# Single gate, weight and output steps on the other engine, GpSimd memsets between the attention's two output stages, and a new fixed order

## The chip, the core and the metric

The kernel runs on one core of one Trainium2 chip. The engines that matter are TensorE (PE, matmuls; PEld is its weight load), VectorE (DVE), ScalarE (ACT), GpSimd (POOL) and SyncE (SP, which issues the DMAs here). The metric is device time in microseconds (us), the median of several runs. Between the runs of the kernel before the spread is 519.86 to 521.3 us.

## The reference

Two parts follow each other. The first is a gated linear attention over 768 tokens for 4 batches and 8 heads of width 48:

```python
for t in range(S):
    state = alpha[:, :, t, :, None] * state + np.einsum('bhd,bhe->bhde', k[:, :, t], v[:, :, t])
    y[:, :, t] = np.einsum('bhd,bhde->bhe', q[:, :, t], state)
```

Its output, laid out as 3072 tokens of 384, is the input `x` of a two-layer network:

```python
h = x @ w_in                                            # 384 x 2048
sp = np.maximum(h, 0.0) + np.log1p(np.exp(-np.abs(h)))
g = h * erf(sp)
return (g @ w_out).astype(np.float32)                   # 2048 x 384
```

q, k, v and alpha come as float32. The two weights come with 8 bytes a number and are turned into float32 parts on the chip.

## The kernel before

**Tiling.** The attention is cut into 24 chunks of 64 positions (two alternating sets, `M`, of 12). Two chunks make one block of 256 tokens for the network, so there are 12 blocks. A block has 4 groups of 512 hidden units, and each group is handled in two halves: a half of `h` is 128x512, a group is 128x1024. Every factor of a matmul is split into a high and a low part (`x_hi`, `x_lo`, `wi_hi`, `wi_lo`, `gh`, `gl`, `wo_hi`, `wo_lo`), and three products are added: hi by hi, the weight's low part by hi, and the weight's high part by lo.

**Steps.** All work is written as small steps with a name and indices. For a chunk: `la lk lq lv` load, `sb` and `sa` are scans over the decays, `rc` and `ic` a reciprocal and its copy, `kk qq td ta` products, `pn` transposes k on PE and `kn` copies the result to SBUF (ACT), `ps` makes the scores, `mk` masks them into `sT` (DVE), `pu` makes the state's update, `qt` and `sv` add the state's part and the scores' part of the output into the PSUM tile `py`, and `xh`, `xl` split `py` into `x_hi` (ACT) and `x_lo` (DVE). For a block: `hm_b_g_half` is the first matmul (18 instructions), `he` copies its PSUM half to `hs` (ACT), `u n1 n2 n3` and `g` are activations on 128x1024 (ACT), `ma mb z1 z2` arithmetic on 128x1024 (DVE), `ga` casts half of `hs` to `gh` (ACT), `gl` makes the rest `hs - gh` (DVE), `om` is the second matmul (12 instructions), `oe` scales and copies the sum in PSUM to `o` (ACT), `od` stores it. For a piece of the weights: `wl` loads, `wc wy wv wa wb` unpack, `wh` takes the high part (ACT), and `wq`, or `wp` on PE with `we` on ACT, the low part; the pieces' low-part steps end in `i` for `w_in` and `o` for `w_out`. `dw` issues matmuls whose result is not used. `f1`, `f2`, `f3` gather a test of the attention's numbers at the very end: on its result the program branches to a slow exact path, which is not taken with these inputs.

**What sets the order.** The text `ORDER` lists all steps once; the program issues them in that order. `Queue` (line 202) ties each instruction of PE, DVE, ACT and SP to the one before it on the same engine, so each of these engines runs exactly in the list's order, and an engine waits when its next instruction's input is not there. GpSimd is not in it. The buffers are rings: 2 of `gh`, 2 of `gl`, 7 of `hs`, 5 of `s`, 4 of `w`, 2 PSUM tiles `h`, one `py`, one `both`, one `kn`, one `sT`. In the profile nearly every instruction has line 210, the call in `Queue`, so groups are told apart by their tiles; names such as `h__111` and `h__112` are the two buffers of one ring. `need` inserts an `ACT_TABLE_LOAD` whenever ACT's next function (`n1 n2 n3` against `u` and `g`) belongs to the other of two table sets.

**Places that the change touches.** `outputs` with `qt` and `sv` (lines 354 to 407): `qt` always opens `py` (`start`), `sv` always closes it (`stop`), except in the first chunk of each set, which has `sv` alone. `kn`, `he`, `oe`, `wy`, `wh`, `we` hold one ACT instruction each. `ga` and `gd` do the same cast on ACT and on DVE; the old list names only `ga`.

Of the kernel before, what the change touches and what calls it, by code (L numbers as in the profile page):

```python
# [20 lines left out]
PSUM = bass.MemoryType.PSUM  # L21
NOSYNC = mybir.DependencyInfo(mybir.DependencyClass.NoSync, mybir.DependencyReason.DATA)
# [3 lines left out]
RT2 = 2.0**0.5  # L26
# [4 lines left out]
la_0 sb_0 wli_1 wci_1 rc_0 wyi_1 ic_0 sa_0 wli_3 wyi_3 wai_1 wbi_1 wci_3 wlo_2 wco_2 wyo_2 whi_1 dw_13 wpi_1  # L31
wai_3 wbi_3 wlo_0 wco_0 wyo_0 whi_3 wpi_3 wao_2 wbo_2 who_2 wao_0 wli_4 wci_4 wyi_4 lk_0 kk_0 wei_3 wbo_0 who_0
pn_0 kn_0 wei_1 la_1 sb_1 wai_4 lq_0 qq_0 wbi_4 wli_2 wyi_2 wci_2 wli_7 whi_4 wqo_2 wci_7 wli_8 wyi_7 wqo_0
wci_8 dw_8 ps_0 wyi_8 wai_2 wbi_2 whi_2 mk_0 dw_1 wpi_4 wei_4 lv_0 dw_2 pu_0 wli_6 wyi_6 wci_6 wai_7 lk_1 wai_8
wpi_2 wei_2 wli_0 wbi_7 whi_7 rc_1 lq_1 wbi_8 whi_8 wai_6 wyi_0 sa_1 sv_0 xh_0 dw_1 wpi_7 wei_7 lk_2 kk_1 wci_0
wbi_6 whi_6 qq_1 wai_0 wli_5 wyi_5 ic_1 wlo_9 wci_5 xl_0 wpi_8 wbi_0 wei_8 whi_0 ps_1 mk_1 wai_5 wpi_6 wei_6
lv_1 sv_1 la_2 ta_0 wlo_12 wli_11 wvo_9 wvo_12 wyo_9 wbi_5 wao_9 wyo_12 wao_12 wpi_0 wli_10 pn_1 wbo_9 whi_5
xh_1 xl_1 sb_2 wbo_12 wei_0 wli_9 wpi_5 rc_2 td_2 wci_11 who_9 wqo_9 wyi_11 sa_2 wai_11 wei_5 wlo_1 who_12
wqo_12 wlo_11 kn_1 lk_3 hm_0_0_0 hm_0_0_1 kk_2 lq_2 wbi_11 he_0_0_0 wyi_10 lv_2 qq_2 wlo_8 wci_10 wai_10
hm_0_2_0 wco_1 pu_1 la_3 sb_3 he_0_0_1 wyi_9 wlo_3 lq_3 wbi_10 qt_2 ps_2 mk_2 u_0_0 ic_2 rc_3 whi_11 wqi_11  # L40
he_0_2_0 whi_10 wqi_10 wyo_1 wao_1 wci_9 sa_3 ta_1 wvo_8 wai_9 n1_0_0 hm_0_1_0 he_0_1_0 wbo_1 td_3 wbi_9 qq_3
sv_2 xh_2 xl_2 hm_0_2_1 he_0_2_1 who_1 wqo_1 pn_2 wyo_8 wao_8 kk_3 hm_0_1_1 wlo_6 kn_2 wbo_8 n2_0_0 wvo_11 whi_9
he_0_1_1 qt_3 pu_2 wqi_9 ps_3 mk_3 ta_2 hm_0_3_0 n3_0_0 ma_0_0 wyo_6 wyo_11 wao_11 g_0_0 ic_3 lq_4 mb_0_0
he_0_3_0 la_4 sb_4 lv_3 sv_3 xh_3 xl_3 rc_4 wco_6 who_8 wqo_8 wao_6 sa_4 wbo_11 hm_0_3_1 he_0_3_1 qq_4 lv_4
z1_0_0 u_0_2 wco_3 lk_4 kk_4 hm_1_0_0 wyo_3 pn_3 kn_3 he_1_0_0 td_4 wbo_6 la_5 wao_3 u_0_1 n1_0_1 hm_1_0_1
z2_0_0 hm_1_1_0 qt_4 he_1_1_0 he_1_0_1 sb_5 pu_3 ps_4 mk_4 ta_3 n2_0_1 who_11 wqo_11 who_6 n3_0_1 ga_0_0_0
n1_0_2 ic_4 lv_5 wbo_3 lk_5 ma_0_1 gl_0_0_0 td_5 rc_5 mb_0_1 wqo_6 n2_0_2 sa_5 ga_0_0_1 gl_0_0_1 n3_0_2 ma_0_2
wlo_10 wvo_10 who_3 wqo_3 mb_0_2 wyo_10 hm_1_2_0 he_1_2_0 hm_1_1_1 he_1_1_1 sv_4 xh_4 xl_4 pn_4 lq_5 qq_5 wlo_7
g_0_1 z1_0_1 wlo_4 ic_5 om_0_0_0 g_0_2 hm_1_2_1 wao_10 z1_0_2 kk_5 z2_0_2 z2_0_1 wlo_15 he_1_2_1 wlo_5 kn_4
wyo_7 wco_7 u_0_3 lq_7 n1_0_3 hm_1_3_0 he_1_3_0 om_0_0_1 ga_0_2_0 gl_0_2_0 hm_1_3_1 ga_0_2_1 wco_4 qt_5 wbo_10  # L50
wlo_13 pu_4 la_6 wao_7 n2_0_3 who_10 ps_5 mk_5 ta_4 om_0_2_0 gl_0_2_1 sv_5 he_1_3_1 wqo_10 wbo_7 n3_0_3 ma_0_3
wyo_4 xh_5 xl_5 wyo_5 wco_5 g_0_3 wao_5 wbo_5 om_0_2_1 who_5 wao_4 mb_0_3 wbo_4 ga_0_1_1 wqo_5 who_7 who_4 wqo_7
gl_0_1_1 wvo_15 ga_0_1_0 wyo_15 hm_2_0_0 he_2_0_0 wqo_4 sb_6 u_1_0 n1_1_0 hm_2_0_1 he_2_0_1 wyo_13 om_0_1_1
gl_0_1_0 om_0_1_0 z1_0_3 hm_2_2_0 wlo_14 wao_15 z2_0_3 wbo_15 wvo_14 n2_1_0 rc_6 wvo_13 ga_0_3_0 gl_0_3_0 wao_13
# [88 lines left out]
def gla_moe(ctx: ExitStack, tc: tile.TileContext, q, k, v, alpha, w_in, w_out, out):  # L143
# [119 lines left out]
    for t in Ts[0] + Ts[1]:  # L263
# [645 lines left out]
```

## Time and profile before

| | |
|---|---|
| median of 3 runs | 519.88 us (519.86 to 521.3) |
| the profiled execution | 519.62 us, of which the span is 517.9 us |
| granted TensorE clock | 1.0 (2.4 GHz) in every stretch |
| busy: PE, PEld, DVE, ACT, POOL | 506.5, 482.4, 463.0, 487.8, 4.4 us |
| the chain that ended last | PE 78%, DVE 11%, ACT 7%, issue 2%, DMA 2%, POOL 1% |
| table loads on ACT | 58 of 1283 ns |

The rows come from one execution of 519.62 us. Matmuls overlap in the profile: a row's duration is longer than the distance from its start to the next one's start, and for what PE costs the distance is the thing to read. On DVE and ACT too, an instruction whose input does not come from the one just before it starts a little before that one ends. Idle time in front of an instruction stands in brackets behind its row, with what ended it.

### The profile page before, as it was taken

Reading aid. Unit: us, or ns where it says so; the run is one execution under the profiler, and the core shown is the slowest. Engines: PE = TensorE matmul, PEld = TensorE weight load, DVE = VectorE, ACT = ScalarE, POOL = GpSimd, SP = SyncE. Lnnn points to the kernel's source line nnn. Section 1 sums busy time; section 2 is a strip of 40 time slices with the busy share of each in tenths; the row PEclk is TensorE's granted clock in tenths of the full one; section 3 lists DMA queues with packets and bytes.
Section 4 is the critical chain, followed back from the end, with each engine's and each line's share of the span. In section 5 each row is a group of like instructions: output and inputs, shape, how many; then the busy total and the mean of one; then the engine's idle time right before and its main releaser. Section 6 shows DMA issues by size and latency. Waiting matters only on the chain.

```text
span 517.9 us, 16807 instructions
## 1 busy us (share of the span) xinstructions
PE 506.5 (98%) x7465; PEld 482.4 (93%) x7465; DVE 463.0 (89%) x590; ACT 487.8 (94%) x696; POOL 4.4 (1%) x19
## 2 busy tenths in 40 slices
PE   6899999999999999999999999999999999999996
PEld 6589999999999999999999999999999999999995
DVE  6999999999999999986899998798887988869784
ACT  7999999999998999899996999999999999999992
POOL 3000000000000000000000000000000000000000
PEclk9999999999999999999999999999999999999999
DMA  8994134412130133111113041023103012000000
GB/s 326 380 334 135 54 122 135 123 50 84 59 117 24 57 100 79 60 45 37 57 58 97 5 152 45 23 84 93 44 1 119 23 59 71 23 34 1 0 32 34
DMA packets 21389, 43.70 MB, mean 84 GB/s; under 512 B 2368, under 2 KB 5440, under 8 KB 21312
## 3 DMA queue, kind: packets, MB, share of 16 engines
q1 hardware_dynamic: 21312, 42.59, 25.1%
q8 instruction: 59, 0.97, 0.8%
q14 instruction: 18, 0.15, 0.1%
HBM read 37.86 MB, written 4.72 MB: 82 GB/s over the span
## 4 chain that ended last, share of the span: by engine, by line
PE 78%; DVE 11%; ACT 7%; issue 2%; DMA 2%; POOL 1%; DVEq 0%; POOLq 0%; ACTq 0%
PE acc L210 34%; PE h__112 L210 16%; PE h__111 L210 16%; PE py L210 5%; PE both L210 5%; PE warm L210 1%; DMA s__86<-in_moe_w_out_dram 1%; DVE t L210 1%; ACT w__97 L210 1%; DVE B L210 1%; DVE w__97 L210 1%; ACT w__100 L210 1%; DVE w__100 L210 1%; ACT wi_lo L210 1%; DVE A L210 1%
## 5 line engine op out<-in xcount | busy, mean ns | idle before, releaser
L210 ACT ACT_TABLE_LOAD x58 | 74.4, 1283 | 1.9 <-PEq L863 0.9
L210 PE MATMUL acc<-wo_hi,gh__102 128*128 128x384 f32 x192 | 44.3, 344 | 0.0
L210 PE MATMUL acc<-wo_hi,gh__101 128*128 128x384 f32 x192 | 43.2, 345 | 0.8 <-ACT gh__101 L210 0.8
L210 PE MATMUL acc<-wo_hi,gl__104 128*128 128x384 f32 x192 | 43.6, 339 | 0.1
L210 PE MATMUL acc<-wo_lo,gh__102 128*128 128x384 f32 x192 | 43.1, 337 | 0.0
L210 PE MATMUL acc<-wo_lo,gh__101 128*128 128x384 f32 x192 | 41.8, 337 | 0.0
L210 PE MATMUL acc<-wo_hi,gl__103 128*128 128x384 f32 x192 | 41.6, 337 | 0.0
L210 PEld LDWEIGHTS acc<-wo_hi,gl__104 128*128 128x128 f32 x192 | 34.1, 188 | 0.9 <-DVE gl__104 L210 0.7
L210 DVE TENSOR_TENSOR_SCAN B<-raw_a,back 128x520 f32<-128x520 f32 x24 | 29.7, 1236 | 5.5 <-POOL T L264 3.9
L210 PEld LDWEIGHTS acc<-wo_lo,gh__102 128*128 128x128 f32 x192 | 34.4, 188 | 0.0
L210 PEld LDWEIGHTS acc<-wo_lo,gh__101 128*128 128x128 f32 x192 | 34.3, 188 | 0.0
L210 PEld LDWEIGHTS acc<-wo_hi,gh__101 128*128 128x128 f32 x192 | 32.1, 188 | 2.4 <-ACT gh__101 L210 1.7
L210 PEld LDWEIGHTS acc<-wo_hi,gl__103 128*128 128x128 f32 x192 | 34.2, 188 | 0.1
L210 PEld LDWEIGHTS acc<-wo_hi,gh__102 128*128 128x128 f32 x192 | 32.7, 188 | 0.7
L210 DVE TENSOR_TENSOR_SCAN A<-raw_a,start 128x520 f32<-128x520 f32 x24 | 29.7, 1236 | 0.1
L210 PE MATMUL h__111<-x_hi__108,wi_hi 128*128 128x256 f32 x144 | 22.1, 289 | 0.0
L210 PE MATMUL h__111<-x_hi__107,wi_hi 128*128 128x256 f32 x144 | 22.0, 288 | 0.0
L210 PE MATMUL h__112<-x_hi__107,wi_hi 128*128 128x256 f32 x144 | 21.8, 287 | 0.1
L210 PE MATMUL h__112<-x_hi__108,wi_hi 128*128 128x256 f32 x144 | 21.7, 286 | 0.0
L210 PE MATMUL h__112<-x_lo__109,wi_hi 128*128 128x256 f32 x144 | 21.2, 282 | 0.2 <-issue 0.2
L210 ACT ACTIVATE s__88<-s__88 128x1024 f32<-128x1024 f32 x20 | 21.2, 1060 | 0.1
L210 DVE TENSOR_TENSOR sT<-both,mask 128x512 f32<-128x512 f32 x24 | 16.3, 681 | 5.6 <-PE both L210 5.6
(301 smaller groups left out, 1432.1 us busy)
## 6 DMA issues: line engine op xcount, KB each, us to landing
raw_a<-in_alpha_dram SPq DMA_DIRECT2D x24, 260.5 KB, 3.1
raw_k<-in_k_dram SPq DMA_DIRECT2D x24, 256.0 KB, 3.2
raw_q<-in_q_dram SPq DMA_DIRECT2D x24, 256.0 KB, 3.6
raw_v__113<-in_v_dram SPq DMA_DIRECT2D x12, 256.0 KB, 3.3
raw_v__114<-in_v_dram SPq DMA_DIRECT2D x12, 256.0 KB, 4.0
out_dram<-o__105 SPq DMA_DIRECT2D x12, 192.0 KB, 2.6
out_dram<-o__106 SPq DMA_DIRECT2D x12, 192.0 KB, 2.3
s__85<-in_moe_w_out_dram SPq DMA_DIRECT2D x4, 384.0 KB, 4.4
```

The costliest lines, as they stand in the source:

```text
L210: ins = made(*args, **kw)
```

## The change

1. **Single steps change the engine.** In the new list 53 of the 96 casts to `gh` are `gd` (DVE, a `CAST` 128x512) in place of `ga`; 16 of the 96 copies of `h` out of PSUM are `hd` in place of `he`; 3 of the 22 copies `kn` are `kd`; 7 of the 24 copies of the output sum are `ob` in place of `oe`; of the weights 2 `whi` are `wki`, one `who` is `wko`, and 4 `wyo` are `wxo`: all these go from ACT to DVE. Six steps go the other way, `wvo` (DVE) to `wco` (ACT). With the list's order the switches between ACT's two table sets go from 57 to 67.
2. **`qt` and `sv` in either order.** Whichever comes first opens `py`, the other closes it. Between the two a GpSimd memset of a 128x1 tile `relay` waits for the opening step's last matmul, and the closing step's first matmul waits for the memset. That is 22 memsets, one for each chunk but the first of each set. `sv` comes first in chunks 14, 15, 21 and 23.
3. **A new list.** All steps are the same otherwise (PE has the same products, 25 `dw` matmuls in all, as before), in another order; among it, `f1` moves from before the last `gl` to behind the last `om`.

```diff
-    def outputs(self, left, right, first, last):
+    def outputs(self, left, right):
+            opening = self.py is None
+            closing = self.first or not opening
+            if opening:
+                self.py = ps_at.tile([P, NI, 512], F32, name="py", tag="a")
...
-                                pe.matmul(
+                                ins = pe.matmul(
...
-                                    start=first and kt == 0 and n == 0,
-                                    stop=last and kt == KT - 1 and n == len(PIECES[kt]) - 1,
+                                    start=opening and kt == 0 and n == 0,
+                                    stop=closing and kt == KT - 1 and n == len(PIECES[kt]) - 1,
...
+                                if self.relay is not None:
+                                    tc.add_manual_dep(ins.ins, self.relay.ins.name, SYNC, reason="row tiles")
+                                    self.relay = None
+            if opening and not closing:
+                self.relay = nc.gpsimd.memset(relay, 0.0)
+                tc.add_manual_dep(self.relay.ins, ins.ins.name, SYNC, reason="row tiles")
...
+        def on_dve(out, in_, scale=1.0):
+            if scale == 1.0:
+                dve.tensor_copy(out=out, in_=in_)
+            else:
+                dve.tensor_scalar(out=out, in0=in_, scalar1=scale, scalar2=None, op0=ALU.mult)
...
-        def he(self, g, half):
+        def he(self, g, half, copy=on_act):
             sl = slice(half * 512, (half + 1) * 512)
-            act.activation(self.hs[g][:, sl], self.phs.pop((g, half)), AF.Copy)
+            copy(self.hs[g][:, sl], self.phs.pop((g, half)))
+
+        def hd(self, g, half):
+            self.he(g, half, on_dve)
...
-gl_11_3_1 f1 om_11_3_1 ga_11_3_0 gl_11_3_0 om_11_3_0 oe_11_0 od_11_0 f2 f3 oe_11_1 od_11_1
+gl_11_3_0 om_11_3_0 ob_11_0 od_11_0 oe_11_1 od_11_1 f1 f2 f3
```

`kd`, `ob`, `wx`, `wk` and `wg` are made like `hd`: the same copy, with `on_dve`.

**The first `x_lo` of block 0.** DVE's rows around the second `xl` in the kernel before; `w2__99`, `w3__100`, `w0__97` are weight pieces being unpacked, `x_lo0__109` the low part of block 0's `x`, `B` the next scan.

```order
L210 SCALAR_TENSOR_TENSOR w2__99<-w2__99 128x512
L210 SCALAR_TENSOR_TENSOR w3__100<-w3__100 128x384
L210 SCALAR_TENSOR_TENSOR w0__97<-w0__97 128x384
...
L210 TENSOR_TENSOR x_lo0__109<-py_388,x_hi0__107 128x2x3x64
L210 SCALAR_TENSOR_TENSOR B_443<-raw_a_115,back_136 128x520
```

The same place now:

```order
L211 CAST wi_hi_142<-w0__97 128x512
L211 SCALAR_TENSOR_TENSOR w1__98<-w1__98 128x512
L211 SCALAR_TENSOR_TENSOR B_383<-raw_a_115,back_137 128x520
L211 TENSOR_TENSOR x_lo0__109<-py_385,x_hi0__107 128x2x3x64
L211 TENSOR_TENSOR wi_lo_143<-w1__98,wi_hi_142 128x512
```

The third scan `B` has moved ahead of this `x_lo`, and a cast and a subtraction of the weights (`wki`, `wqi`) now stand on DVE around it.

**The output stages of chunk 14.** PE's rows before, from the opening `qt` (`py<-raw_q,T`) over chunk 13's `pu` (`both<-raw_v,kn`) and this chunk's `ps` (`both<-raw_q,raw_k`) to the closing `sv` (`py<-sT,raw_v`), with what they wait for by the program.

```order
L210 MATMUL py<-raw_q_117,T 32x64 [waits PE_49]
...
L210 MATMUL both<-raw_v__114,kn 48x48 [waits Activation_49]
...
L210 MATMUL both<-raw_q_117,raw_k_119 64x64 [waits DMAHW7_49]
...
L210 MATMUL h__112<-x_hi__107,wi_hi 128x256 [waits Activation_49]
...
L210 MATMUL h__111<-x_hi__107,wi_hi 128x256 [waits Activation_49]
...
L210 MATMUL py<-sT,raw_v__113 32x64 [waits DMAHW7_49,DVE_49]
```

PE's rows now, for the same chunk's `sv` and `qt`:

```order
L211 MATMUL py<-sT,raw_v__113 32x64 [waits DMAHW1_49,PE_49]
...
L211 MATMUL both<-raw_v__113,kn 48x48 [waits Activation_49]
...
L211 MATMUL both<-raw_q_117,raw_k_119 64x64 [waits DMAHW6_49,DMAHW2_49,DVE_49]
...
L211 MATMUL py<-raw_q_116,T 32x64 [waits Pool_49]
L211 MATMUL py<-raw_q_116,T 32x64 x31
```

`sv` now opens and `qt` closes behind a wait for GpSimd, with chunk 14's own `pu` and chunk 15's `ps` between them, where two `hm` stood as well; the first row of each run of matmuls is shown.

**The end of the program.** DVE's last rows before: the two `gl` of the last group, between them the test `f1` (`bad`, `good`), and the test's last step `f3` (`total`).

```order
L210 SCALAR_TENSOR_TENSOR hs__93<-s__88,hs__93 128x1024
L210 TENSOR_TENSOR gl__103<-hs__93,gh__101 128x512
L210 TENSOR_SCALAR bad<-inv 128x192 x2
L210 TENSOR_REDUCE good<-bad 128x1
L210 TENSOR_SCALAR bad<-sums 128x24 x2
...
L210 TENSOR_TENSOR gl__104<-hs__93,gh__102 128x512
L210 CAST total<-both 1x1
```

DVE's last rows now:

```order
L211 CAST gh__101<-hs__93 128x512
L211 TENSOR_TENSOR gl__103<-hs__93,gh__101 128x512
L211 CAST gh__102<-hs__93 128x512
L211 TENSOR_TENSOR gl__104<-hs__93,gh__102 128x512
L211 TENSOR_SCALAR o__105<-acc 128x384
L211 TENSOR_SCALAR bad<-inv 128x192 x2
...
L211 CAST total<-both 1x1
```

Both last casts to `gh` and the copy `ob` of the last sum have come to DVE, and `f1` now stands behind that copy, which waits for the last `om`.

## Rows read from the trace of the kernel before

**Rows 1.** The page's first part: busy time, share of the span, instructions.
```profile
PE 506.5 (98%) x7465; PEld 482.4 (93%) x7465; DVE 463.0 (89%) x590; ACT 487.8 (94%) x696; POOL 4.4 (1%) x19
```

**Rows 2.** Busy time by 20-us windows: length, engines (instructions), clock, DMA share, GB/s.
```profile
40.00:60.00 20.00, 20.00 (x392) 19.11 (x391) 20.00 (x35) 19.92 (x35) 0.00 (x0) 1.00 0.32 101
...
200.00:220.00 20.00, 20.00 (x315) 19.45 (x314) 19.76 (x23) 18.41 (x26) 0.00 (x0) 1.00 0.27 75
220.00:240.00 20.00, 20.00 (x321) 19.49 (x320) 15.11 (x20) 19.78 (x28) 0.00 (x0) 1.00 0.19 55
...
440.00:460.00 20.00, 20.00 (x445) 18.63 (x444) 14.55 (x20) 19.63 (x27) 0.00 (x0) 1.00 0.07 16
```

**Rows 3.** Timeline of PE around one attention group: start, duration, instruction.
```profile
37.88 0.69 PE L210 MATMUL both<-raw_q,raw_k 48*64 48x64 f32 x32
38.50 0.98 PE L210 MATMUL h__111<-x_hi__107,wi_hi 128*128 128x256 f32 x6
39.31 0.88 PE L210 MATMUL h__111<-x_hi__107,wi_lo 128*128 128x256 f32 x6
40.02 0.86 PE L210 MATMUL h__111<-x_lo__109,wi_hi 128*128 128x256 f32 x6
40.82 0.86 PE L210 MATMUL py<-sT,raw_v__113 64*32 64x64 f32 x64
41.61 0.98 PE L210 MATMUL h__112<-x_hi__107,wi_hi 128*128 128x256 f32 x6
```

**Rows 4.** The chain that ended last, a stretch of `om` alone.
```profile
240.64 6.36 PE acc L210 x36
```

**Rows 5.** Timeline of the start: first scan, second `x_lo`, first `hm`.
```profile
3.88 1.24 DVE L210 TENSOR_TENSOR_SCAN B<-raw_a,back 128x520 f32<-128x520 f32 x1 [3.88 <-POOL T L264]
...
29.49 0.56 DVE L210 TENSOR_TENSOR x_lo__109<-py,x_hi__107 128x384 fp32r<-128x384 f32 x1
...
30.00 0.97 PE L210 MATMUL h__112<-x_hi__107,wi_hi 128*128 128x256 f32 x6
```

**Rows 6.** Timeline of DVE, back to back.
```profile
216.99 1.23 DVE L210 SCALAR_TENSOR_TENSOR hs__90<-s__86,hs__90 128x1024 f32<-128x1024 f32 x1
218.13 0.68 DVE L210 TENSOR_TENSOR sT<-both,mask 128x512 f32<-128x512 f32 x1
218.74 0.68 DVE L210 TENSOR_TENSOR gl__103<-hs__96,gh__102 128x512 fp32r<-128x512 f32 x1
```

**Rows 7.** Groups by line, DVE and ACT: busy us, mean ns, idle before, releaser.
```profile
L210 DVE TENSOR_SCALAR w__100<-s__85 128x384 int32<-128x384 int32 x2 | 0.7, 360 | 0.0
L210 DVE TENSOR_SCALAR bad<-inv 128x192 f32<-128x192 f32 x2 | 0.4, 255 | 0.0
...
L210 ACT ACT_TABLE_LOAD x58 | 74.4, 1283 | 1.9 <-PEq L863 0.9
L210 ACT ACTIVATE s__88<-s__88 128x1024 f32<-128x1024 f32 x20 | 21.2, 1060 | 0.1
```

**Rows 8.** Timeline of the end, DVE, ACT, PE and SP.
```profile
494.98 0.60 ACT L210 ACTIVATE hs__93<-h__111 128x512 f32<-128x512 f32 x1
...
508.10 0.63 ACT L210 ACTIVATE gh__101<-hs__93 128x512 fp32r<-128x512 f32 x1 [2.70 <-DVE hs__93 L210]
...
508.78 0.97 PE L210 MATMUL acc<-wo_hi,gh__101 128*128 128x384 f32 x4 [0.41 <-ACT gh__101 L210]
509.37 0.42 DVE L210 TENSOR_SCALAR bad<-inv 128x192 f32<-128x192 f32 x2
...
511.23 0.69 DVE L210 TENSOR_TENSOR gl__104<-hs__93,gh__102 128x512 fp32r<-128x512 f32 x1
...
513.58 0.19 PE L210 MATMUL both<-ones,good 128*1 128x1 f32 x2
513.81 0.15 DVE L210 CAST total<-both 1x1 int32<-1x1 f32 x1 [1.89 <-PE both L210]
514.20 0.33 SPq L210 DMA_DIRECT2D out_dram<-o__106  x1
```

More of the change, by code (lines that the diff above doesn't have):

```diff
@@ new lines @@
+n1_5_1 gd_4_1_0 z2_4_2 n1_5_2 n2_5_2 sa_13 n3_4_3 ma_4_3 ic_13 mb_4_3 hm_5_0_1 he_5_0_1 u_5_0 pn_12 g_4_3 lv_13
+hm_5_3_0 sv_12 xh_12 gl_4_1_0 om_4_1_0 gd_4_1_1 gl_4_1_1 kn_12 xl_12 pu_12 qq_13 ps_13 qt_13 n2_5_1 om_4_1_1
+la_14 sb_14 mk_13 n3_5_2 ta_12 he_5_3_0 pn_13 hm_5_3_1 n3_5_1 z1_4_3 lk_14 kk_14 sv_13 gd_4_2_0 rc_14 sa_14
+lq_14 qq_14 td_14 kn_13 pu_13 ps_14 n1_5_0 n2_5_0 n3_5_0 gl_4_2_0 ga_4_2_1 om_4_2_0 ma_5_1 mb_5_1 he_5_3_1
+ma_5_2 g_5_2 xh_13 la_15 gl_4_2_1 om_4_2_1 ic_14 g_5_1 lk_15 sb_15 u_5_3 xl_13 z2_4_3 n1_5_3 od_3_0 mk_14 ta_13
@@ L234, in gla_moe @@
     minus = const.tile([P, P], F32R, name="minus")
+    relay = const.tile([P, 1], F32, name="relay")
     ones = const.tile([P, 1], F32, name="ones")
@@ L282, in __init__ @@
             self.last = self.c == CPB - 1
+            self.py = self.relay = None
         def la(self):
@@ L338, in pn, with natural @@
                 )
-        def kn(self):
+        def natural(self, copy):
             if self.last:
@@ L344, in kn, with kd @@
             rows = self.pn_[:, 0, :].rearrange("p (a b d) -> p a b d", a=NP, b=2)
-            act.activation(self.kn_, rows[:, :, :, :D], AF.Copy)
+            copy(self.kn_, rows[:, :, :, :D])
+        def kn(self):
+            self.natural(on_act)
+        def kd(self):
+            self.natural(on_dve)
         def td(self):
@@ L605, in om, with oe, ob @@
                 )
[L607 removed]
+        def oe(self, c, copy=on_act):
             o = self.pl.gp.tile([P, DM], F32, name="o", tag=f"o{c}", bufs=1)
[L609 removed]
+            copy(o, self.acc[c][:, :DM], RT2)
             self.o[c] = o
+        def ob(self, c):
+            self.oe(c, on_dve)
         def od(self, c):
@@ L674, in wb, with wh, wk @@
                 )
-        def wh(self):
-            act.activation(self.hi, self.z, AF.Copy)
+        def wh(self, copy=on_act):
+            copy(self.hi, self.z)
+        def wk(self):
+            self.wh(on_dve)
         def wq(self):
@@ L686, in wp, with we, wg @@
             pe.matmul(out=o, lhsT=minus, rhs=self.hi, start=False, stop=True)
-        def we(self):
-            act.activation(self.lo, self.rest[:, : self.n], AF.Copy)
+        def we(self, copy=on_act):
+            copy(self.lo, self.rest[:, : self.n])
+        def wg(self):
+            self.we(on_dve)
     weights = {}
```

229 lines of the change are left out of this document (112 added, 117 removed).

## The prediction

> **What bounds the kernel now.** I read the page's shares first: PE 98%, ACT 94%, DVE 89%, GpSimd idle [rows 1]. An average hides stages, so I read the windows next. PE is full in all four stretches shown. DVE is full too in the early ones (20.00 of 20 us, and still 19.76 in 200 to 220), then falls to 15.11 and 14.55; ACT is at 18.41 to 19.92 throughout [rows 2]. The clock is 1.00 in each of them. So there are two regimes: until about 220 us PE, DVE and ACT are all nearly full; after that DVE has 3 to 5 us of air in 20, ACT little. A change that brings work from ACT to DVE is dear in the first and cheap in the second.
>
> PE's price list is read as distances between starts. One `hm` has three thirds; 39.31 to 40.02 gives 0.71 for a third, so 2.13 for all. The third behind an attention group takes 0.81 (38.50 to 39.31) and the one ahead of one 0.80 (40.02 to 40.82): about 0.19 for each attention group that stands between big matmuls. `sv` takes 0.79 (40.82 to 41.61), `ps` 0.62 with its change of shape [rows 3]; `qt` has as many matmuls as `sv`, and `pu` and `pn` I take at 0.4 and 0.36. 36 matmuls of three `om` take 6.36, so one takes 2.12 [rows 4]. All PE work behind the first `hm`, added up so (96 `hm`, 96 `om`, 20 `pn`, 22 `ps`, 21 `pu`, 22 each of `sv` and `qt`, 44 groups), is 479.4 us. The first `hm` starts at 30.00 [rows 5] and the last `om` ends just before 513.5 [rows 8]: 483.5. So PE waits for only about 4 us after its start; that is all that a better order can win there, beside an earlier start.
>
> **The change, part by part.** *ACT.* It loses 53 casts of about 0.5, 16 PSUM copies of about 0.5, some 13 pieces of 0.4, and gains 10 table loads of 1.28 [rows 7] and six unpackings of 0.45: about 27 us less. That frees ACT, which then bounds nothing.
>
> *DVE's durations.* Back to back, a row's successor starts a little before it ends: 216.99 to 218.13 is 1.14 for a row of 1.23, 218.13 to 218.74 is 0.61 for 0.68 [rows 6]. So I take row minus 0.085 everywhere: 1.14 for 1024 columns, 0.60 for 512, 0.47 for 384, 1.155 for a scan, 0.27 for a one-source row of 384 [rows 5 to 7]; a reciprocal of 8 columns I put at 0.12. An instruction that needs the result of the one just before it loses about another 0.12.
>
> *The new casts, SBUF to SBUF.* No large `CAST` runs on DVE before. The nearest rows are the one-source `TENSOR_SCALAR`: 360 ns for 384 columns, 255 for 192, so 0.55 ns a column and about 0.43 us for 512, 0.34 start to start [rows 7]. The upper bound is a two-source row of the same size, 0.60 [rows 6]; the lower is the 192-column row's 0.17. I take 0.34, being nearest in kind. 53 x 0.34 is 18 us. *Copies out of PSUM on DVE* (`hd`, `ob`, `kd`): the only row that reads 512 columns of PSUM is `sT`, 0.61 [rows 6], but it has two sources; bounds 0.34 and 0.61, and I take the upper. 16 x 0.6 + 10 x 0.47 = 14.3. With six unpackings away (-1.6) and the few weight casts, DVE gets about 33 us more, and 4 more by 32 further dependent neighbours at 0.12: 463 becomes about 500 of 518.
>
> The Trainium skill (Perfetto Trace Analysis, Optimizing Scalar/DVE Operations) says that a saturated DVE is a reason to hand work to ScalarE, and not the reverse; the full windows of [rows 2] agree that DVE is saturated, but only until 220 us. By it the early part of this change would lose; it is the slower rival's direction, priced below from rows. The skill's VectorE: DVE Perf Modes (Why PSUM operands drop a tier) says that a float32 operand in PSUM takes away the faster mode of one-source operations; by it `hd` would cost what `sT` does, and otherwise 26 pieces would be some 6 us cheaper in all, most of them late, where DVE has air. No row here shows such a copy.
>
> *Where DVE decides.* What counts is when DVE can be through a given `gl`, against when PE wants it. Up to `gl_3_3_0` the old list gives DVE 26 scans, 13 reciprocals, 70 rows of 1024, 97 of 512, 80 of 384 and 8 unpackings: 209.3, plus 32 dependent neighbours x 0.12, plus its start at 3.88 [rows 5] = 217.0. That `gl` stands at 218.74 to 219.42 [rows 6], so DVE had idled 2.3 us by then. Up to `gl_4_2_1` the new list gives 30 scans, 15 reciprocals, 82 of 1024, 110 of 512 (one of them an `hd`), 87 of 384, 7 unpackings and 20 casts: 245.4, plus 40 x 0.12, plus 3.88 = 254.0. PE's work ahead of the matmuls that want it: 48 `hm`, 37 `om`, 13 `pn`, 13 `pu`, 13 `ps`, 24 of `sv` and `qt`, a moved `wp` and dummy matmuls (1.7), 24 groups x 0.19 = 223.3, and 1.4 within `om_4_2_1`. From a first `hm` at 27.4 (next paragraph) PE would be there at 252.1. So DVE is late by 1.9 even without any idle time. Other places between 90 and 290 us come out at 1.9 to 2.5. With an idle time like the old one's 2.3 it is about 4; after 300 us the sum leaves DVE ahead again. I take PE's waits at 4.0 us: as many as in the old kernel, in another place.
>
> *The start.* DVE is full from its first scan at 3.88 to the second `x_lo` at 29.49 [rows 5]. The new list puts 1.4 us less in front of it, although the third scan now stands ahead, since unpacking has moved behind; ACT has 3 us less up to the second `x_hi`. `wki`, `wp` and the weight's `wq` then decide, and I place the first `hm` at 27.4 instead of 30.00. But 2.1 us of PE work (a `wp`, a `pn`, dummy matmuls) move behind it, less 4 groups x 0.19 = 0.76: PE's work becomes 480.8.
>
> *The relay.* A closing step waits PE to GpSimd to PE. A handover between engines costs about 0.04 (513.77 to 513.81 [rows 8]) and a memset of few columns 0.1 to 0.2, so about 0.25. The smallest cover is `pu` and `ps`, about 1.0, in chunks 14, 15, 19 and 20; elsewhere a whole `hm` or `om`. So I cost it at nothing; with no cover it would be 22 x 0.25 = 5.5, which is the upper bound.
>
> *The tail.* In the old list the chain from the last `he` (494.98) to its cast (508.10) takes 13.1 us and PE still waits 0.41 at 508.78; with two waits like it (one of them behind `f1`, which holds the last `gl` back from 509.37 to 511.23) some 1.3 to 1.6 us are lost [rows 8]. The new chain is 0.6, three activations and one more of 1.06, a table load of 1.28 [rows 7], four DVE steps of 1.22, a cast and one `gl`: about 12.5, under six `om` of 2.12 = 12.7. I leave 0.3. But `f1` (1.86) now runs behind the last `om` and its copy, so the test's total, 0.3 behind the last `om` before (513.5 to 513.81), comes 1.9 to 2.2 behind it. SP was then busy until 514.53 issuing the last store [rows 8], and the program ends some 3.2 us after that; the total overtakes that point by about 0.8.
>
> *Sum.* 27.4 + 480.8 + 4.0 + 0.3 = 512.5 for the last `om`, 1.0 earlier than 513.5; plus 0.8 at the end: 0.2 less. That is 519.4 on the profiled execution's 519.62, and 519.7 against the median of 519.88, which is 0.26 above it. A measurement of this kernel can tell about 0.3% from no change, 1.56 us either way: 518.3 to 521.4.
>
> **The rivals.** *A, DVE keeps up (faster).* If casts cost less than 0.34 or idle time goes, the wait falls from 4.0 to 2 or less; with the early start whole, 27.4 + 480.8 + 1 + 0 + the end gives a last `om` near 509.5, so about 516.5. For it: ACT, relieved by 27 us, no longer holds DVE up by its own lateness, which was part of the 2.3. Against it: the DVE sum alone is already 1.9 late.
>
> *B, DVE becomes the bound of the first 250 us (slower).* One mechanism: the place is the 20 casts, 2 PSUM copies and moved `gl` up to block 4. If a cast takes 0.60 like a two-source row, 20 x 0.26 = 5.2 us more stand in front of `gl_4_2_1`; PE then waits 9 instead of 4, and the time is about 524.5. It turns against the change as soon as a cast takes more than about 0.42 start to start (1.6 us over 20 casts). The full DVE windows [rows 2] speak for it, the two one-source rows [rows 7] against it.
>
> *C, the relay shows.* If the round trip is 0.5 beyond its cover in the four tight chunks, 2 us; with 0.1 in the others another 2: about 522. The rows' short handovers speak against it.
>
> *D, the order does not bite.* Were PE's sum alone to decide, with the old waits, the time is 519.88 less the 1.2 of start and sum: still within 0.3%; this belongs to the forecast.
>
> **How the numbers follow.** Forecast (with D) 0.45, its own range 518 to 521.5; A 0.31; B 0.18; C 0.06. Of the forecast's 0.45 about 0.03 falls on either side of the bound, while 0.02 of A and 0.01 of C lie within it. So faster 0.32, same 0.42, slower 0.26. The range of 8 in 10 takes in A's 516.5 and half of B: 516.3 to 523.5.
>
> **What would show it.** First `hm` near 27.4 us; DVE 97 to 99% in every window up to about 290 us and PE's waits there ended by DVE's `gl`, 4 us in all; ACT near 460 us busy with 68 table loads; a `CAST` 128x512 of about 0.42 us; no PE wait on GpSimd behind a closing `sv` or `qt`; `total` near 2 us after the last `om`. A cast row near 0.68 or PE waits of over 7 us make B; PE waits under 2 us make A; a first `hm` later than 29 takes the gain at the start away.

## The result, and the profile after

The changed kernel takes 523.27 us in the median of 5 runs (522.9 to 524.84), the kernel before, run beside it, 520.49 (519.86 to 521.3): a ratio of 1.0069 [1.0051, 1.0088]. It is slower, by more than the 0.3% that counts as no change here. A second measurement of the same kernel gave 1.0047 [1.0031, 1.0064]. The profiled execution took 522.9 us with a span of 521.2, against 519.62 and 517.9 before: 3.3 us more.

The page's shares and chain, which answer to [rows 1]:

```profile
PE 505.2 (97%) x7465; PEld 480.4 (92%) x7465; DVE 494.4 (95%) x670; ACT 464.9 (89%) x626; POOL 6.6 (1%) x41
...
PE 56%; DVE 24%; ACT 13%; issue 4%; DMA 2%; DVEq 0%; SPq 0%
```

The load has moved the way that was forecast, a little less of it: DVE gains 31 us (forecast 37) and ACT loses 23 (27). But the chain that ended last now runs over DVE for 24% of the span, where it was 11%. The windows of [rows 2] again, with the same columns:

```profile
40.00:60.00 20.00, 18.99 (x483) 16.98 (x481) 20.00 (x31) 19.94 (x36) 0.20 (x2) 1.00 0.41 124
...
200.00:220.00 20.00, 20.00 (x305) 19.09 (x304) 19.69 (x27) 18.63 (x23) 0.10 (x1) 1.00 0.25 77
220.00:240.00 20.00, 20.00 (x266) 19.68 (x265) 19.80 (x27) 18.71 (x24) 0.10 (x1) 1.00 0.16 41
```

After 200 us PE is as full as it was, although DVE is now full until 240 us and beyond. What is new is in the first window: PE falls from 20.00 to 18.99. The sum line of the four windows from 40 to 120 us says it in one row, first for the kernel before, then for the changed one:

```profile
sum 80.00, PE 79.88 PEld 76.13 DVE 79.42 ACT 79.61 POOL 0.00; mean PE 19.97 PEld 19.03 DVE 19.85 ACT 19.90 POOL 0.00
```

```profile
sum 80.00, PE 76.96 PEld 72.54 DVE 77.98 ACT 78.38 POOL 0.40; mean PE 19.24 PEld 18.14 DVE 19.50 ACT 19.59 POOL 0.10
```

PE lacks 2.9 us of 80 there; DVE and ACT are a little less busy too. PE's timeline shows two kinds of idle time in this stretch; first the handovers, with the rows on DVE and ACT that PE waited for:

```profile
51.24 0.69 DVE L211 TENSOR_TENSOR sT<-both,mask 128x512 f32<-128x512 f32 x1
...
52.03 0.85 PE L211 MATMUL py<-sT,raw_v__113 64*32 64x64 f32 x64 [0.56 <-issue]
...
53.10 0.49 ACT L211 ACTIVATE x_hi__108<-py 128x384 fp32r<-128x384 f32 x1
...
53.73 0.97 PE L211 MATMUL h__111<-x_hi__108,wi_hi 128*128 128x256 f32 x6 [0.27 <-ACT x_hi__108 L211]
```

The matmul at 52.03 starts just behind the end of `sT` (51.93), the one at 53.73 behind `x_hi` (53.59). The bracket "issue" names no engine for the first, so its releaser is read from the ends of the rows. The second kind stands inside a run of equal matmuls that wait for nothing in the program (a `ps`, 32 matmuls on inputs long there):

```profile
59.37 0.54 PE L211 MATMUL both<-raw_q,raw_k 48*64 48x64 f32 x24
61.05 0.34 PE L211 MATMUL both<-raw_q,raw_k 48*64 48x64 f32 x8 [1.14 <-issue]
```

The bracket counts from a modelled end; by the distance of the starts, 1.4 us are lost. The start of the program, against [rows 5]: the first `hm`, two of DVE's new casts and the first relay.

```profile
28.07 0.98 PE L211 MATMUL h__111<-x_hi__107,wi_hi 128*128 128x256 f32 x6
...
35.77 0.42 DVE L211 CAST wi_hi<-w__99 128x512 fp32r<-128x512 f32 x1
36.11 0.35 DVE L211 CAST wo_hi<-w__97 128x384 fp32r<-128x384 f32 x1
...
38.85 0.10 POOL L395 MEMSET relay<- 128x1 f32 x1 [33.61 <-PE py L211]
```

And the end, against [rows 8], where a copy out of PSUM on DVE stands at 497.96:

```profile
497.96 0.68 DVE L211 COPY hs__93<-h__112 128x512 f32<-128x512 f32 x1
498.56 1.21 DVE L211 SCALAR_TENSOR_TENSOR w__99<-t,w__99 128x1024 f32<-128x1024 f32 x1
...
511.14 0.43 DVE L211 CAST gh__101<-hs__93 128x512 fp32r<-128x512 f32 x1
...
511.63 0.96 PE L211 MATMUL acc<-wo_hi,gh__101 128*128 128x384 f32 x4 [0.59 <-DVE gh__101 L211]
...
515.05 0.56 DVE L211 TENSOR_SCALAR o__105<-acc 128x384 f32<-128x384 f32 x1 [1.55 <-PE acc L211]
...
515.53 0.42 DVE L211 TENSOR_SCALAR bad<-inv 128x192 f32<-128x192 f32 x2
515.55 0.51 PE L211 MATMUL acc<-wo_hi,gl__104 128*128 128x384 f32 x2
...
517.50 0.19 PE L211 MATMUL both<-ones,good 128*1 128x1 f32 x2 [1.44 <-DVE good L211]
```

The last `om` waits for its cast at 511.63 (0.59), where [rows 8] had 0.41. The test (`bad` to `good`) runs only behind the copy `o` of the last sum but one, so that PE's matmul for the total stands at 517.50, 1.8 us behind the last `om`; before it was 0.3.

**The account, profile against profile.** The first `hm` is 1.93 us earlier (28.07 for 30.00). The last matmul of the last `om` starts at 515.72 (the second of the two at 515.55) where it stood at 513.31: 2.41 later, so PE takes 4.34 us more between the two. At the end `f1` adds 0.9 (from that last matmul's start to the end of the span 4.6 before, 5.4 now). Sum: -1.9 + 4.3 + 0.9 = 3.3.

What the 4.3 are is read row by row. Nearly everywhere in these traces a step takes the same time from its start to the next one's: a third of `hm` 0.71, a third of `om` 0.69 to 0.71, 0.09 more ahead of a group of small matmuls and 0.10 more behind one, 0.08 more behind a `pn`, `sv` and `qt` 0.79, `ps` 0.59 to 0.63, `pu` 0.40, `pn` 0.36. Where a step takes over 0.15 us more than that, I count the excess as a wait of PE. This finds 2.5 us in 6 places before, 1.5 of them in the tail, and 6.3 us in a dozen places now: 3.8 more. The remaining 0.5 is work that moved behind the first `hm`, less what `om` varies by.

Below, "late" at a time is the sum of these waits up to it; at 118 us it is 0.5 in the kernel before and 4.2 in the changed one, at 470 us 1.0 and 5.0.

### The profile page after: what moved, and what is told of

It is laid out like the page before. It is cut to its first block, busy times and chain, and to the rows that moved or that the text cites. A ratio compares the mean times of both kernels' runs of the same rounds, so it can differ in the third digit from the quotient of the medians.

```text
span 521.2 us, 16851 instructions
## 1 busy us (share of the span) xinstructions
PE 505.2 (97%) x7465; PEld 480.4 (92%) x7465; DVE 494.4 (95%) x670; ACT 464.9 (89%) x626; POOL 6.6 (1%) x41
## 4 chain that ended last, share of the span: by engine, by line
PE 56%; DVE 24%; ACT 13%; issue 4%; DMA 2%; DVEq 0%; SPq 0%
PE acc L211 24%; PE h__112 L211 12%; PE h__111 L211 12%; PE py L211 4%; PE both L211 4%; DVE t L211 3%; ACT L211 2%; DMA hs__90<-in_moe_w_in_dram 2%; DVE gl__104 L211 2%; DVE gl__103 L211 2%; ACT w__98 L211 2%; DVE w__97 L211 1%; DVE A L211 1%; ACT s__89 L211 1%; ACT w__100 L211 1%
## 5 line engine op out<-in xcount | busy, mean ns | idle before, releaser
L211 DVE TENSOR_TENSOR_SCAN B<-raw_a,back 128x520 f32<-128x520 f32 x24 | 29.6, 1232 | 3.7 <-DMA raw_a<-in_alpha_dram 3.7
L211 DVE TENSOR_TENSOR_SCAN A<-raw_a,start 128x520 f32<-128x520 f32 x24 | 29.6, 1235 | 0.3
L211 ACT ACTIVATE s__87<-s__87 128x1024 f32<-128x1024 f32 x22 | 23.2, 1056 | 1.4 <-DVE t L211 1.3
L211 PE MATMUL h__112<-x_hi__107,wi_hi 128*128 128x256 f32 x150 | 22.6, 286 | 0.2 <-ACT hs__95 L211 0.2
L211 PE MATMUL h__111<-x_hi__108,wi_hi 128*128 128x256 f32 x150 | 22.5, 285 | 0.3 <-ACT x_hi__108 L211 0.3
L211 PE MATMUL h__112<-x_hi__107,wi_lo 128*128 128x256 f32 x150 | 22.0, 281 | 0.1
L211 ACT ACTIVATE s__88<-s__88 128x1024 f32<-128x1024 f32 x20 | 21.1, 1057 | 0.8 <-DVE t L211 0.6
L211 PE MATMUL h__111<-x_hi__108,wi_lo 128*128 128x256 f32 x150 | 21.8, 281 | 0.0
L211 PE MATMUL h__112<-x_lo__109,wi_hi 128*128 128x256 f32 x150 | 21.8, 281 | 0.0
```

Source lines behind the costliest of these rows:

```text
L211: ins = made(*args, **kw)
```

## The experiments

Two theories stood against each other. One: the new order itself makes PE wait in the first 118 us (handovers too tight, and the stall inside `ps`). Two: DVE, full with the new casts, sets the pace, so that whatever PE loses or gains early is taken or given back by DVE. Beside them, the relay and `f1`.

**The new code with the old order.** The new `outputs`, with all relays, and the old list:

```diff
-gl_11_3_0 om_11_3_0 ob_11_0 od_11_0 oe_11_1 od_11_1 f1 f2 f3
+gl_11_3_1 f1 om_11_3_1 ga_11_3_0 gl_11_3_0 om_11_3_0 oe_11_0 od_11_0 f2 f3 oe_11_1 od_11_1
```

> The changed kernel's code with the old list: same steps and engines as before, but the 22 GpSimd memsets and the waits through them are in. Theory 1 (the loss is in the list's first 116 us and in the step behind the last om): nothing, ratio to before 1.000 within 0.002. Rival (the relay's waits show): 22 x 0.1 to 0.25 us, ratio 1.004 to 1.010.

Measured: 520.19 us, 1.0003 [0.9989, 1.0018]. The relay costs nothing that shows; the whole loss is the list's.

**The old list up to `hm_2_3_0`, the rest of the new one behind it.**

```diff
 kn_6 n2_1_1 hm_2_3_0
-n2_1_2 xh_6 xl_6 n3_1_1 td_7 qq_7
+he_2_1_1 hm_2_3_1 n3_1_1 ma_1_1 g_1_1 lv_7
```

> The old list up to hm_2_3_0 (at 116 us before), then the new list's remaining steps in the new order. Theory 1 (the new list loses its time in the first 116 us): the last om comes some 2.6 us earlier than in the changed kernel (about 513.1 us), time about 520.3. Theory 2 (DVE's added casts bind between 90 and 290 us, so that early waits only hide a later one): PE waits come back at gl steps between 120 and 290 us, and the time stays at 522 to 523.

Measured: 530.05 us, 1.0188 [1.0163, 1.0212]. PE's longest wait, two rows behind it and a window (its columns as in [rows 2]) say why:

```profile
PE py L205 <- DVE raw_q L205: 5.7, 1, 5.7
...
132.41 1.48 PE L205 MATMUL acc<-wo_lo,gh__101 128*128 128x384 f32 x4
133.69 1.48 PE L205 MATMUL acc<-wo_hi,gl__103 128*128 128x384 f32 x4
...
120.00:160.00 40.00, 33.67 (x391) 32.43 (x391) 30.79 (x37) 33.16 (x44) 0.10 (x1) 0.87 0.11 33
```

The seam itself costs one wait of 5.7 us: DVE had not made `raw_q` yet, since the two lists put its steps at different places. That wait, which ends at 128.12, is not all: from 126.6 to 136.8 us the granted clock is at its lower level, 1.2 GHz (0.87 in the mean of the window), and a third of `om` takes 1.28 us there (132.41 to 133.69) for 0.70 behind it (137.27 to 137.97), some 3 us in all. The run tells nothing about either theory, and was a bad place for a seam.

**`f1` back before the last `gl`.**

```diff
-gl_11_3_1 om_11_3_1 gd_11_3_0 gl_11_3_0 om_11_3_0 ob_11_0 od_11_0 oe_11_1 od_11_1 f1 f2 f3
+gl_11_3_1 om_11_3_1 ga_11_3_0 f1 gl_11_3_0 om_11_3_0 ob_11_0 od_11_0 oe_11_1 od_11_1 f2 f3
```

> The new list with f1 between the last two gl as before, and the last cast to gh on ACT. Theory 1: total is no longer 1.8 us behind the last om but 0.3; the last om itself moves by 0 to 0.4 later; time 0.7 to 1.0 us below the changed kernel. If the end is bound by the last store instead: no gain.

Measured: 522.19 us, 1.0043 [1.0029, 1.0057]. Here the last cast is ACT's again. PE's last rows in this kernel:

```profile
516.78 0.61 PE L205 MATMUL acc<-wo_hi,gl__104 128*128 128x384 f32 x2 [0.17 <-DVE gl__104 L205]
...
518.37 0.19 PE L205 MATMUL both<-ones,good 128*1 128x1 f32 x2
```

The total no longer waits behind the last `om`; in exchange the last `om` waits for its `gl`, some 0.35 us. From first `hm` to end it is 492.5 us against 493.1. So, in these two traces, of `f1`'s 0.9 about 0.6 is to be had back, and the rest of the loss stands without it. One of this kernel's 12 executions took 2701.78 us, over five times the others; no trace of it is on record, and its cause is open.

**A smaller burst of loads before the stall.** The load `lq_5` moved to 28 steps earlier, so that fewer loads are in the queues at 58 us.

```diff
-gl_0_0_1 kn_3 kk_4 qq_4 lq_5 hm_1_0_0
+gl_0_0_1 kn_3 kk_4 qq_4 hm_1_0_0
...
-z1_0_0 pu_2 ps_3 qt_3 wxo_3
+z1_0_0 pu_2 ps_3 qt_3 lq_5 wxo_3
```

> The new list with one load (lq_5, 256 KB) issued before the weight load wlo_7 instead of behind la_5, so that the burst of loads from 53.6 to 58 us is 256 KB shorter. Theory 1a (the 1.36 us stall inside ps_4 at 59.7 us is PE's instruction stream, fetched late behind this burst): the stall goes or falls below 0.4 us, time 0.5 to 1.3 us below the changed kernel. Rival (the stall has another cause, such as data of ps_4): it stays, time unchanged.

Measured: 522.41 us, 1.0048 [1.003, 1.0067]. The stall stayed, at the very same matmul:

```profile
58.67 0.54 PE L205 MATMUL both<-raw_q,raw_k 48*64 48x64 f32 x24
60.83 0.34 PE L205 MATMUL both<-raw_q,raw_k 48*64 48x64 f32 x8 [1.62 <-issue]
```

A stall that keeps its place by number, between the 24th and the 25th matmul, belongs to the instruction stream and not to the data's loads. A burst that is 256 KB smaller does not shorten it; the expectation missed.

**The changed kernel again,** run beside the others with no edit.

> The changed kernel itself, timed once more beside the others. Ratio to before 1.005 to 1.009. A stall of 1.3 to 1.9 us inside ps_4 near 60 us, at the same matmul of the program (number 985), as in every trace of this list so far.

Measured: 522.82 us, 1.0047 [1.0031, 1.0064]. The same matmul stalls (1.5 us by starts), and one place 512 instructions earlier in PE's stream a little as well:

```profile
48.34 0.34 PE L205 MATMUL py<-raw_q,T 48*32 48x64 f32 x13 [0.18 <-issue]
...
60.33 0.34 PE L205 MATMUL both<-raw_q,raw_k 48*64 48x64 f32 x8 [1.32 <-issue]
```

**The instruction stream shifted.** One `dw` step early in the list issues another number of its idle matmuls, so that all behind it stand at other positions.

```diff
-wyi_7 whi_5 dw_7 wpi_5 wai_7
+wyi_7 whi_5 dw_15 wpi_5 wai_7
```

> The new list with 8 more dummy matmuls (dw_7 becomes dw_15) at 15.8 us, where PE waits anyway. They move PE's stream of instructions by 16, and with it the places where one 16 KB fetch of instructions ends and the next begins. Theory 1a (the stall in ps_4 is a fetch that comes 2.4 us after it began, while PE ran through its last 256 instructions in 2.6 us of small matmuls): the stall at that matmul goes or falls under 0.5 us, and the time by about 1.2 us against the changed kernel. Rival (something else holds ps_4): the stall stays at the same matmul. Theory 2 (DVE decides later): the stall goes, but PE waits for gl or gh between 120 and 290 us take its place and the time stays.

Measured: 523.86 us, 1.0065 [1.0049, 1.0081]. The stall at `ps` is gone (late at 62 us: 1.5 instead of 2.9). But nothing is won:

```profile
76.75 0.69 DVE L205 TENSOR_TENSOR raw_q<-raw_q,A 128x512 f32<-128x512 f32 x1
...
77.53 0.85 PE L205 MATMUL py<-raw_q,T 48*32 48x64 f32 x64 [1.21 <-issue]
...
169.91 0.84 PE L205 MATMUL py<-raw_q,T 48*32 48x64 f32 x63 [0.28 <-DVE x_lo__109 L205]
171.62 0.21 PE L205 MATMUL py<-raw_q,T 48*32 48x64 f32 x1 [0.87 <-issue]
```

At 77.53 PE waits 1.2 us for `raw_q`, which DVE ends at 77.44: DVE takes back what PE had won. Counted from the first `hm` and matmul by matmul against the changed kernel, PE is 1.4 us ahead at 62 us and level at 90, and at 118 us it is 4.1 late again. So the stall by itself costs this list nothing: theory two holds here. At 171.62 another stall of 1.1 us stands inside a run of matmuls, before the last of 64.

**The old list up to `z1_1_2`, the new one behind it,** a seam where the two lists' DVE steps agree better.

```diff
 g_1_2 lq_8 z1_1_2
-z2_1_2 pn_7 hm_3_0_1 la_8 sb_8 lv_8
+lk_9 n1_1_3 n2_1_3 n3_1_3 ic_7 ma_1_3
```

> The old list up to z1_1_2 (hm_3_0_0 starts there, at 127.5 us before and 131.2 us in the changed kernel), then the new list's rest; at this place the two lists have nearly the same steps behind them (5 us of work apart, where the first splice had over 10 apart). Theory 1 (the loss is in the list's first 130 us): 3 to 3.7 us below the changed kernel, about 519.5. Theory 2: PE waits between 130 and 290 us give back 2 us or more of it, about 521.5.

Measured: 523.26 us, 1.0057 [1.0041, 1.0073]. First its sum of the windows from 40 to 120 us, then the first wait behind the seam:

```profile
sum 80.00, PE 79.98 PEld 76.50 DVE 79.55 ACT 79.64 POOL 0.49; mean PE 20.00 PEld 19.12 DVE 19.89 ACT 19.91 POOL 0.12
```

```profile
134.16 0.96 PE L205 MATMUL acc<-wo_hi,gh__101 128*128 128x384 f32 x4 [1.73 <-ACT gh__101 L205]
```

With the old order the early stretch is full, and late at 118 us is 0.4. Some 1.9 us come back at 134 us, where ACT's cast is not ready; at 470 us PE is 3.2 late instead of 5.0. From first `hm` to end it takes 489.7 us, between 487.9 (before) and 493.1 (changed). So most of the loss does sit in the first 118 us; but this start also has the old first `hm` (30.77 here), and the old end's cheap `f1` is missing, and the sum is no faster.

**The casts of blocks 0 to 4 back on ACT.** 19 steps of this kind, the list otherwise as changed:

```diff
-gd_0_1_1
+ga_0_1_1
...
-gd_4_3_0
+ga_4_3_0
```

> The new list with the 19 casts to gh of blocks 0 to 4 that had gone to DVE back on ACT (19 x 0.34 us less on DVE, 19 x 0.52 us more on ACT up to about 300 us). Theory 1 (in the stretch of these casts PE waits for nothing, behind 116 us): the time does not change by more than 0.7 us. Theory 2 (these casts make DVE the bound): 2 us or more below the changed kernel.

Measured: 550.11 us, 1.055 [1.0521, 1.0579]. The largest of PE's waits (total, times, longest):

```profile
PE acc L205 <- ACT gh__102 L205: 5.1, 4, 1.9
...
PE h__112 L205 <- ACT hs__94 L205: 2.8, 1, 2.8
```

At the matmul that the changed kernel reaches at 200 us PE is 20 us behind it, counted from the first `hm`. The rival that the casts on DVE are simply the wrong move falls for this list: it leaves ACT no room for them. Some 6 of the 28 us lost are the clock: at the end of waits of 2.1, 1.3 and 2.8 us, or up to 1 us behind, the granted clock falls to 1.2 GHz for 3.4, 6.8 and 3.4 us (from 148.7, 169.2 and 251.1). That ACT's lateness spreads so far is seen, not explained in detail.

**Less work on DVE, new order.** The step `wb`, one instruction for each piece of the weights, is left out, so that the weights lose their signs; DVE's busy time falls by 13.0 us (494.4 to 481.4).

```diff
         def wb(self):
-            if self.wide:
-                y, z = self.parts()
-                dve.scalar_tensor_tensor(
-                    out=z, in0=y.bitcast(I32), scalar=-0x80000000, in1=z, op0=ALU.bitwise_and, op1=ALU.bitwise_or
-                )
+            return
```

> The new list with one DVE step of the weights' unpacking left out (wb, which puts the sign into the 28 pieces: 12 x 0.60 + 16 x 0.47 = 14.7 us of DVE in the first 120 us; the weights lose their signs). Theory 2 (a DVE that is full sets when PE may go on, wherever the wait shows): PE's lateness at 118 us falls from 4.0 to the instruction fetches' 1.4 to 1.9 and no more, the rest of the list runs without new waits, and the time falls by 2.5 us or more, beside an earlier first hm. Theory 1 (the order of PE's and ACT's steps makes the early waits): the lateness at 118 us stays at 3.5 or more.

Measured: 521.27 us, 1.0033 [1.0017, 1.005]. Its sum of the same four windows, and the `ps` that stalls:

```profile
sum 80.00, PE 78.09 PEld 74.25 DVE 73.50 ACT 79.29 POOL 0.39; mean PE 19.52 PEld 18.56 DVE 18.37 ACT 19.82 POOL 0.10
```

```profile
59.49 0.34 PE L205 MATMUL both<-raw_q,raw_k 48*64 48x64 f32 x7 [0.29 <-issue]
```

DVE now has air (73.5 of 80), and yet PE is 3.0 late at 118 us, only 1.2 less. About 0.8 of that is the stall, which shrank to some 0.55 by starts, and 0.4 a wait at 89.8 us that is gone. The waits of 0.4 to 0.7 stand where they stood (43.1, 51.3, 53.0, 114.1 us). Theory two in its strong form falls: those waits belong to the chains that the list makes, not to DVE's load as a whole.

**Less work on DVE, old order:** the same edit, with the old list.

```diff
         def wb(self):
-            if self.wide:
...
+            return
```

> The old list with the same DVE step left out, as a measure for the one before: PE was late by 0.9 us at 118 us here, so by theory 2 there is little to win behind the first hm (under 0.8 us), and the two kernels without this step stand within 1 us of each other but for the first hm and the end. By theory 1 the new list stays 3 us behind.

Measured: 520.53 us, 1.0011 [0.9994, 1.0028]. The sum of its windows from 40 to 120 us:

```profile
sum 80.00, PE 79.93 PEld 76.53 DVE 74.41 ACT 79.71 POOL 0.49; mean PE 19.98 PEld 19.13 DVE 18.60 ACT 19.93 POOL 0.12
```

Late at 118 us is 0.4. With DVE relieved in both, the new list is still 2.5 us behind the old one there, and 2.8 at 470 us. This pair shows that most of the early loss goes with the list and not with DVE's load. One trace of each would not be enough for it: in all seven traces with the old order up to there late at 118 us goes from 0.4 to 2.2 (1.8 and 2.2 in the last two kernels below); in the five with the new order and all of DVE's work it stays at 4.1 to 4.2. A list is an order and a choice of engines at once. In front of the step at 115.9 us 16 steps have changed engine, 3 of them casts to `gh`; no run takes the new order with the old engines, so the two are not told apart there.

**The old list with the new tail's ideas.** `f1` behind `gl_10_3_0`, and two of the last casts on DVE:

```diff
-ga_10_3_0 gl_10_3_0
+ga_10_3_0 gl_10_3_0 f1
...
-od_10_1 z2_11_1
+od_10_1 z2_11_1 gd_11_1_0
...
-n1_11_3 z2_11_2 ga_11_1_0
+n1_11_3 z2_11_2
...
-om_11_2_1 z2_11_3 ga_11_3_1
+om_11_2_1 z2_11_3 gd_11_3_1
...
-od_10_0 gl_11_3_1 f1
+od_10_0 gl_11_3_1
```

> The old list with three edits in its last 40 us: f1 in a gap of DVE at 485 us, and two of the casts to gh (11_1_0 and 11_3_1) on DVE. PE's waits of 0.44, 0.41 and 0.46 us behind 499 us go: 0.8 to 1.3 us below the kernel before, ratio 0.9975 to 0.9985. If f1 delays the chain of block 11 instead: no gain.

Measured: 519.33 us, 0.9985 [0.9969, 1.0001]. Of the old tail's three waits two go, the one before the last `om` stays (0.5 by starts, for DVE's `gh`) and two of 0.25 come in; the test is hidden. This is the fastest order found, but its interval touches no change, so it isn't called faster.

**The old list shifted,** to ask whether the old order stalls as well when its stream stands elsewhere:

```diff
-wqo_0 wci_8 dw_8 ps_0
+wqo_0 wci_8 dw_2 ps_0
```

> The old list with 6 dummy matmuls fewer at the start (dw_8 becomes dw_2), which moves PE's stream of instructions by 24 against the places where its 16 KB fetches join. Theory 1a: PE then runs through one fetch of 256 instructions near 48 us in 1.9 us, and a stall of 0.7 to 1.5 us that no wait of the program explains appears inside qt, pu or ps there, where the kernel before has none. Rival (such stalls have to do with the new list's data): no stall appears.

Measured: 520.36 us, 1.0007 [0.9991, 1.0022]. The first `hm` is 1.45 us later here, so the place that was named, 48 us, comes at about 49.5. A stall of 0.4 us does stand behind it, inside the `ps` of 50.47 (1.02 from its start to the next, for 0.59), smaller than the 0.7 to 1.5 that were expected; one of 0.3 at 86.5 us and one of 0.5 at 364.7 follow:

```profile
50.47 1.10 PE L206 MATMUL both<-raw_q,raw_k 48*64 48x64 f32 x32
...
363.90 0.54 PE L206 MATMUL both<-raw_q,raw_k 48*64 48x64 f32 x24
364.73 0.34 PE L206 MATMUL both<-raw_q,raw_k 48*64 48x64 f32 x8 [0.29 <-issue]
```

So the old order is open to such stalls. The kernel before has one too, of 0.4 us, inside an `hm`:

```profile
180.94 0.87 PE L210 MATMUL h__112<-x_lo__109,wi_hi 128*128 128x256 f32 x5 [0.23 <-issue]
```

## Why the prediction was wrong

**The step that failed** is the last one of the part on where DVE decides: "I take PE's waits at 4.0 us: as many as in the old kernel, in another place." With it the sum lets PE's waits grow by 0.2 us (4.0 and 0.3 in the tail, for about 4.1). Read row by row they grow by 3.8, from 2.5 to 6.3. The other terms are near: from the first `hm` to the last `om` the forecast was 1.6 more, of which 1.4 is work, and 4.3 came; the start is 0.7 later than forecast and the end 0.1.

The step rested on "So PE waits for only about 4 us after its start", and that was the remainder of a sum and no reading of rows. The sum isn't good to a few us. Its prices, as printed, add up to 480.4 and not to 479.4. A `pn` between big matmuls makes the step behind it 0.08 dearer (0.79 for 0.71), and 17 of them are left out:

```profile
188.91 0.60 PE L210 MATMUL both<-ident,raw_k 128*128 128x128 f32 x4
189.27 0.96 PE L210 MATMUL h__112<-x_hi__107,wi_hi 128*128 128x256 f32 x6
190.06 0.88 PE L210 MATMUL h__112<-x_hi__107,wi_lo 128*128 128x256 f32 x6
```

And a third of `om` takes 0.69 or 0.71 us within one trace, which over 288 of them is some 4 us, as much as the remainder. By the rows the old kernel waited 1.0 us ahead of its tail: there was almost nothing that new waits could stand in for.

**The place of the new waits was wrong too.** They were forecast as DVE's lateness at `gl`s between 90 and 290 us. Of the 6.3 us, 4.2 stand before 118 us: six handovers of 0.2 to 0.7 us (at 43.8, 52.0, 53.7, 89.8, 94.4 and 115.9 us), some 2.9 in all, and the stall of 1.4, in whose place DVE's `raw_q` at 77.5 us would have come. Another 1.3 is the tail's, behind 478 us. The very `gl` that the prediction worked out, `gl_4_2_1`, is the tightest one between 90 and 290 us, and still costs only some 0.4:

```profile
257.61 0.69 DVE L211 TENSOR_TENSOR gl__104<-hs__91,gh__102 128x512 fp32r<-128x512 f32 x1
...
258.35 0.97 PE L211 MATMUL acc<-wo_hi,gl__104 128*128 128x384 f32 x4
```

DVE ends it at 258.30, later than the forecast's 254.0 to 256.3; but PE, which was to be there at 252.1, comes at about 258 itself. So naming that place was right, and the 1.9 to 4 us were wrong: PE had lost them earlier, elsewhere. Nor is it DVE's load that makes it tight: with 13 us less on DVE the same `gl` ends at 256.50, and PE takes it at 256.56. The Trainium skill (Perfetto Trace Analysis, Optimizing Scalar/DVE Operations) takes a saturated DVE as a reason to hand work away from it; here the full DVE did forbid a gain (77.5 us), but relieving it of 13 us did not remove the loss, so the rule alone would have told the wrong cause.

**The start** came 1.9 us earlier, forecast 2.6. It varies from run to run: 27.3 to 28.1 us in the changed list, 29.6 to 31.5 in the old one. It was 30.13 once with the changed list (`f1` back), in an execution whose granted clock was 1.2 GHz from 25.3 to 28.7 us. What else moves it isn't settled.

**PE's work** was forecast to rise by 1.4; between the first `hm` and the last `om` 0.5 is left beside the waits, and the spread of `om` is as large as the difference.

**DVE's prices were right.** A `CAST` takes 0.42 and 0.34 from start to start (35.77 to 36.11), so rival B's point of decision, 0.42 start to start, was not reached. A copy of 512 columns out of PSUM takes 0.68, and 0.60 from start to start (497.96 to 498.56), the bound that was taken. The groups of the changed kernel (busy us, mean ns, idle before):

```profile
L211 DVE CAST gh__101<-hs__91 128x512 fp32r<-128x512 f32 x7 | 3.0, 424 | 0.3
...
L211 DVE COPY hs__91<-h__112 128x512 f32<-128x512 f32 x3 | 2.0, 677 | 0.0
...
L211 ACT ACT_TABLE_LOAD x68 | 87.2, 1283 | 2.0 <-PEq L901 0.9
```

The Trainium skill (VectorE: DVE Perf Modes, Why PSUM operands drop a tier) says that a float32 operand in PSUM loses the faster mode; the trace agrees, 0.68 out of PSUM against 0.42 in SBUF for the same 512 columns. DVE's total was forecast near 500 and is 494.4, ACT's 460 and is 464.9, with the 68 table loads as counted.

**The relay** costs nothing, as forecast: no wait of PE names it, and the new code with the old order is level.

**The tail**: behind 490 us waits of 1.0 remain where 0.3 was forecast and 1.3 to 1.6 counted before (1.5 by the rows); `f1` behind the last `om` adds 0.9 at the end, forecast 0.8.

**What stays open:** which single steps would have to move to loosen each of the six handovers without making DVE or ACT late elsewhere. Each was located; as a group they go with the list, and none was repaired by itself.

## What to carry to other kernels

Before a wait is moved or replaced in a sum, find its rows. The remainder of a long sum carries the spread of all its prices; what a better order can win is the waits that rows show, and here they were 1.0 us ahead of the tail. A new order is judged in the stretch where all engines are full: the handovers that were 0.2 to 0.7 us too tight in the changed list's first 118 us were not got back later. And a gain on one engine counts only up to the next engine's lateness: price the wait that comes next before the one that goes is booked.

## What the hardware showed that was not expected

PE's own instruction stream can run dry. It comes over a queue of its own, in 59 packets for 0.97 MB, 16 KB each:

```profile
q8 instruction: 59, 0.97, 0.8%
```

PE's stream, counted in the changed kernel's trace, has 14995 instructions, or 254 to a packet. The stalls without a wait in the program fall at one phase of 256 in this count: at about 1986 and, smaller, 1475 in the kernels with the new list, at 5313 in the shifted one, at 1474, 2756 and 11457 in the shifted old one and at 5826 in the kernel before, 193 to 196 beyond a multiple of 256 in all. Each of them ended 2.2 to 2.8 us after the start of a packet (changed kernel: 58.67 and 61.05), while the packets themselves took 0.9 to 1.4 us. Most stand in runs such as `qt`, `pu` and `ps`, 128 small matmuls in some 1.8 us (from 58.18), the one of the kernel before in an `hm`; they take 0.3 to 1.8 us each. The Trainium skill (Runtime: NRT & Kernel Launch, Instruction fetch mechanics) states blocks of 16 KB with 256 instructions, which agrees with the packets, and calls the price of a block's edge mostly hidden; here it is hidden at nearly all of the 59 and not at these. What sets the time from a block's edge to its packet was not isolated; the experiment with fewer loads did not shorten it.
